# A scheduled attention and FFN kernel: batch 0's FFN spread later, batch 2's attention in two rounds

## The chip, the cores and the metric

One NeuronCore of one Trainium2 chip. The metric is device time in microseconds (us) of one execution, as the median of several runs. Engines: PE is TensorE (its weight loads are shown apart as PEld), DVE is VectorE, ACT is ScalarE, POOL is GpSimd, SP is SyncE, which here issues all DMAs.

## What is computed

Eight batches of attention with 8 heads, 576 positions and head size 64, in which a score counts only if it is within `tau` of its row's maximum, and behind it a two-layer FFN (512 to 2048 to 512, SiLU between) over all 4608 rows, in float32:

```python
scores = scale * np.matmul(q, k.transpose(0, 1, 3, 2))
thresh = np.max(scores, axis=-1, keepdims=True) - tau
scores = np.where(scores >= thresh, scores, -1000000000.0)
attn = softmax(scores)
x = (attn @ v).transpose(0, 2, 1, 3).reshape(B * S, H * D)
h = x @ w_in
g = h * (1.0 / (1.0 + np.exp(-h)))
out = g @ w_out
```

## The kernel before

**Tiles.** Attention goes by tiles of 128 score rows against all 576 keys of a head; the two heads of a pair share the tile with the last 64 rows of each. There are 36 tiles a batch and 288 in all; in this text they are counted from 0. Per tile: PE writes scores (L468; L456 in batch 0), DVE takes the row maximum (L478), ACT the exponential (L488), DVE masks and sums (L497), the tile is scaled by the inverse sum (L515 on ACT or L511 on POOL), POOL splits it into two halves of float16 (`hl`, L523, L526, L529), and SP transposes it by DMA into `wT` (L539). Batch 0 instead transposes on PE (`tm` L407, `tl` L412) and copies the result out on ACT (L420, L421). When a head pair is done, PE multiplies by the values (L554; L430 in batch 0) and `av_post` writes the FFN's input `x16` (L572 on ACT, L573 on DVE).

**Rounds.** A batch either runs all its tiles pair by pair (kind `all`, query columns 0 to 287 and 288 to 575 as FFN ranges) or in two rounds over the four pairs: `low` with 256 query columns (4 tiles a pair) and `high` with the other 320 (5 tiles a pair). Two rounds let the FFN of the first range begin when the first round is done. Batch 0 always does this; batches named in `HALVED` (L41) do too. In each round of a halved batch a head's queries and keys are loaded (`load_qk`, L338 and L339, through SP) and split: keys on ACT and POOL (`split_k`, L362 and L364), queries on ACT and DVE (`split_q`, L353 and L354; only the round's columns).

**FFN units.** A range of columns gives 16 h units (12 matmuls of the first layer, L597, then L607, L608, L614, L615 on ACT and DVE in turn, into `gbuf`) and 16 o units (12 matmuls of the second layer, L630; every fourth is followed by an output copy L642 on ACT and its DMA L644). The ranges of batch 0, and the first of batch 1, list their h units before their o units; later ranges pair their h units with the o units of the range before.

**Pacing.** The main loop counts steps t, one per tile, with 12 empty steps (`GAP`) between batch 0's two rounds and one (`GAP1`) before batch 1; a tile's number is t less the empty steps before it. At each step it adds `rate` to a credit and emits one FFN unit for each whole credit. `rate` is set when a range becomes ready: for batch 0 from `RATES` (1.03 after the first round, 1.45 after the second), later so that the units in the list are 95% done when the next range comes.

**Scheduler.** The instructions are not run in the order of the loop. A scheduler with its own timing model sets each engine's order, by priorities that put scores, soft-max and the value product ahead of FFN units. `keep_in_program_order` pins the first matmul of a unit behind whatever PE instruction the loop emitted just before it; it is used for batches below `PACED` (L34).

Of the kernel before, what the change touches and what calls it, by code (L numbers as in the profile page):

```python
# [30 lines left out]
LOAD = 5  # L31
AV_LAG = 3
GAP, GAP1 = 12, 1
PACED = 1  # L34
RATES = (1.03, 1.45)
RATE = 0.95

W_PLAN = ((0, 0, 10, 13, 0), (16, 9, 22, 36, 0))
PRI_S, PRI_SOFT1, PRI_SOFT2 = 1600, 50, 200
PRI_AV = 1500  # L40
HALVED = (1,)  # L41

# [8 lines left out]
def attention_moe(  # L53
# [198 lines left out]
    def load_v(b, p):  # L252
        t = sb.tile([P, 2, 5, D], F32, tag="vraw", name=f"vraw_{b}_{p}", bufs=5)
        nc.sync.dma_start(out=t, in_=vL[b, :, 2 * p : 2 * p + 2])
        vraw[b, p] = t
# [3 lines left out]
    def vmax(b, p):  # L259
        if b == 0:  # L260
            if p == 0:
                vps.append(bank([P, P], "vps_0", 2))
            flat = vraw[b, p].rearrange("p o k d -> p (o k d)").bitcast(BF16)
            upper = flat.rearrange("p (c t) -> p c t", t=2)[:, :, 1]
            for j in range(5):
                part = upper[:, j * P : (j + 1) * P]
                nc.tensor.matmul(
                    vps[0], part, part, start=(p == 0 and j == 0), stop=(p == 3 and j == 4)
                )
            if p == 3:  # L270
                vmx[b] = const.tile([P, 1], F32, name="vmx_0", tag="vmx0")
                nc.vector.tensor_reduce(out=vmx[b], in_=vps[0], op=ALU.max, axis=AX.X)
            return
        if p == 0:
            vmx[b] = const.tile([P, NPAIR], F32, name=f"vmx_{b}", tag="vmx")
        nc.vector.tensor_reduce(
            out=vmx[b][:, p : p + 1], in_=vraw[b, p], op=ALU.max, axis=AX.XYZ,
            apply_absolute_value=True,
        )
# [31 lines left out]
    def split_v(b, p):  # L311
        t = vraw[b, p]
        s = vsc[b][:, 0:1]
        o = sb.tile([P, 2, 2, 5, D], F16, tag="v16", name=f"v16_{b}_{p}", bufs=4)
        nc.scalar.activation(o[:, 0], t, AF.Copy, scale=s)
        nc.vector.scalar_tensor_tensor(
            out=o[:, 1], in0=t, scalar=s, in1=o[:, 0], op0=ALU.mult, op1=ALU.subtract
        )
        v16[b, p] = o
# [124 lines left out]
    def scores(t):  # L444
        v, parts = tiles[t]
        s_ps = ps_s.tile([P, 2, 512], F32, tag="s", name=f"s_{t}")
        sps[t] = s_ps
        if v in direct:
            (h, i, _, _) = parts[0]
            qt, kt = direct[v]  # L450
            if visits[v][2] == "low":
                o = (h % 2) * 256 + i * P
            else:
                o = (h % 2) * 384 + (i - 2) * P
            for j in range(2):
                nc.tensor.matmul(  # L456
                    s_ps[:, j, :HALF], qt[:, o : o + P],
                    kt[:, j * HALF : (j + 1) * HALF], start=True, stop=True,
                )
            return  # L460
        seq = [
            (qstack[h % 2][:, qcol(h, i) : qcol(h, i) + P], kk)
            for h, i, _, _ in parts
            for kk in khl[h]
        ]
        for n, (lhs, kk) in enumerate(seq):
            for j in range(2):
                nc.tensor.matmul(  # L468
                    s_ps[:, j, :HALF], lhs, kk[:, j * HALF : (j + 1) * HALF],
                    start=(n == 0), stop=(n == len(seq) - 1),  # L470
                )

    def soft1(t):
        s_ps = sps[t]
        sm = sb.tile([P, 5], F32, tag="small", name=f"sm_{t}", bufs=4)
        w = sb.tile([P, S], F32, tag="w32", name=f"w32_{t}", bufs=4)
        negm = sm[:, 0:1]
        nc.vector.tensor_reduce(  # L478
            out=negm, in_=s_ps[:, :, :HALF], op=ALU.max, axis=AX.XY, negate=True
        )  # L480
        nc.vector.tensor_scalar(
            out=sm[:, 1:2], in0=negm, scalar1=-1.0, scalar2=ntau, op0=ALU.mult, op1=ALU.add
        )
        small[t] = sm
        wtile[t] = w
# [104 lines left out]
    def h_unit(b, c0, n, f, own=None):  # L590
# [4 lines left out]
        for c in range(NK):  # L595
            for lo_w, lo_x in ((0, 0), (0, 1), (1, 0)):
# [3 lines left out]
                )  # L600
                if b < PACED and k == 0:
                    tc.keep_in_program_order(mm)
# [20 lines left out]
    def o_unit(b, c0, n, d, quarter, own=None):  # L623
# [3 lines left out]
        for f in range(4 * quarter, 4 * quarter + 4):  # L627
            g = gt[b, c0, f]
            for k, (lo_w, lo_g) in enumerate(((0, 0), (0, 1), (1, 0))):
# [3 lines left out]
                )  # L633
                if b < PACED and f == 4 * quarter and k == 0:
                    tc.keep_in_program_order(mm)
# [12 lines left out]
    def h_units(b, c0, n, owns=(None,)):  # L648
        return [
            lambda f=f: h_unit(b, c0, n, f, owns[f % len(owns)]) for f in range(NF)  # L650
        ]

    def o_units(b, c0, n, owns=(None,)):
        return [
            lambda d=d, quarter=quarter: o_unit(b, c0, n, d, quarter, owns[d % len(owns)])
            for d in range(DM // P) for quarter in range(4)
        ]
# [3 lines left out]
    def moe_units(b, c0, n):  # L661
        if b == 0 and c0 == 0:
            return h_units(b, c0, n, (0, 2)) + o_units(b, c0, n, (0, 2))
        if b == 0 or (b == 1 and c0 == 0 and 1 in HALVED):
            return h_units(b, c0, n) + o_units(b, c0, n)
        out = []
        if held:
            for pair in zip(h_units(b, c0, n, (0, 1)), o_units(*held.pop(), (2,))):
                out.extend(pair)
        else:  # L670
            out = h_units(b, c0, n)
        held.append((b, c0, n))
        return out
# [3 lines left out]
    for b in range(1, B):  # L677
        for kind in ("low", "high") if b in HALVED else ("all",):
            visits += [(b, p, kind) for p in range(NPAIR)]
    todo = {}  # L680
    def at(t, f):
        todo.setdefault(t, []).append(f)
# [42 lines left out]
    for b in range(B):  # L725
        u = start[b, 0]
        for p in range(NPAIR):
# [3 lines left out]
            elif b == 1:  # L731
                at(u + 5 * p - 20, lambda p=p: load_v(1, p))
                at(u + 5 * p - 15, lambda p=p: vmax(1, p))
                at(u + (4 if 1 in HALVED else 9) * p + 4, lambda p=p: split_v(1, p))
            else:
                pace, first = (4, 24) if b in HALVED else (9, 40)
                at(u + pace * p - first, lambda b=b, p=p: load_v(b, p))
# [4 lines left out]
    def pri(offset, f):  # L742
        def g():
            if offset == 0:
                return f()
            with tc.high_priority(offset=offset):
                return f()

        return g
# [25 lines left out]
    rate = 0.0  # L775
# [6 lines left out]
    def step_unit():  # L782
        p = units.pop(0)()
        run_posts()
        post.append(p)

    def live(t):
        return 0 <= t < NT and tiles[t] is not None
# [3 lines left out]
    while t < NT + 8 or units or ready or held:  # L792
        while ready and ready[0][0] <= t:
            _, b, c0, n = ready.pop(0)
            units.extend(moe_units(b, c0, n))
            nxt = [r[0] for r in ready if r[0] > t + 1]
            rate = len(units) / max(1, (nxt[0] if nxt else NT + 8) - t)
            rate *= RATE
            if b == 0:
                rate = RATES[0 if c0 == 0 else 1]  # L800
        if held and not ready and not units and t >= NT + 8:
            units.extend(o_units(*held.pop()))
        if t >= first_high + 20:
            turn[1] = 3
        if live(t):
            pri(PRI_SOFT1, lambda: soft1(t))()
        if live(t + 1):
            pri(PRI_S, lambda: scores(t + 1))()
        if live(t - 1):
            soft2b(t - 1)  # L810
        if live(t):
            pri(PRI_SOFT1, lambda: soft1b(t))()
        if live(t - 1) and tiles[t - 1][0] not in direct:
            soft3(t - 1)
        if live(t - 2) and tiles[t - 2][0] in direct:
            soft3(t - 2)
        for f in todo.pop(t, []):
            f()
        credit += rate
        if t >= NT:  # L820
            credit = max(credit, 4.0)
        if units and credit >= 1:
            step_unit()
            credit -= 1
        if live(t):
            pri(PRI_SOFT2, lambda: soft2(t))()
        for v, p, c0, n in avs.pop(t, []):
            b = visits[v][0]
            if v in direct:
                a_ps = av_direct(v, p)  # L830
            else:
                a_ps = pri(PRI_AV, lambda v=v, p=p, c0=c0, n=n: av(v, p, c0, n))()
            run_posts()
            scale = xscale if v in direct else 2.0**-12
            post.append(lambda b=b, p=p, c0=c0, n=n, a_ps=a_ps, scale=scale: av_post(b, p, c0, n, a_ps, scale))
        while units and credit >= 1:
            step_unit()
            credit -= 1
        if not units:
            credit = 0.0  # L840
            run_posts()
        t += 1
# [44 lines left out]
```

## Time and profile before

| | us |
|---|---|
| median of three timed runs (1227.8 to 1229.81) | 1228.99 |
| the profiled execution | 1226.58 |
| its span, first to last instruction | 1224.8 |
| PE busy | 1155.2 (94%) |
| DVE busy | 920.7 (75%) |
| ACT busy | 808.4 (66%) |
| POOL busy | 694.6 (57%) |

Busy shares are averages over stages with different limits, so the span is cut into stages at tile boundaries. A row of a stage gives the time in which each engine was busy; what is missing to the stage's length is idle time of that engine. The idle time of the engine that sets the end is what can be won.

### The profile page before, as it was taken

What the parts mean: (1) busy time and instruction counts of PE and PEld (TensorE: products, weight loads), DVE (VectorE), ACT (ScalarE), POOL (GpSimd) and SP (SyncE); (2) the same over time, 40 slices, a digit from 0 to 9 for tenths busy, and PEclk for the clock granted to TensorE, in tenths of its full rate; (3) what the DMA queues carried; (4) which work ended last, traced back from release to release, by engine and by line L of the source; (5) the groups of instructions that cost most, each with busy time, mean ns of one, the idle gap of its engine ahead of it and who ended that gap; (6) DMA issues with size and microseconds to landing.
All of it is one profiled execution on the core that took longest, in us unless ns stands there. A gap on an engine that the chain in (4) does not pass through costs nothing.

```text
span 1224.8 us, 27015 instructions
## 1 busy us (share of the span) xinstructions
PE 1155.2 (94%) x9474; PEld 902.3 (74%) x9474; DVE 920.7 (75%) x2625; ACT 808.4 (66%) x1519; POOL 694.6 (57%) x888
## 2 busy tenths in 40 slices
PE   6778998999999899999999999999999999999998
PEld 4546685777876677777877777787788877777777
DVE  7987949968989788899888888896788867333330
ACT  6679846967868676777777677785777756333331
POOL 2264226987877786877878658781787567000000
PEclk9999999999999999999999999999999999999999
DMA  9740127787896787787777748772888357100000
GB/s 313 264 133 28 51 58 180 155 167 159 152 172 128 168 148 136 146 154 172 142 145 145 162 96 171 142 136 82 137 159 141 84 103 122 26 11 16 15 11 25
DMA packets 340887, 151.73 MB, mean 124 GB/s; under 512 B 305936, under 2 KB 317200, under 8 KB 340752
## 3 DMA queue, kind: packets, MB, share of 16 engines
q1 hardware_dynamic: 340752, 150.01, 57.9%
q8 instruction: 75, 1.23, 0.4%
q14 instruction: 60, 0.49, 0.1%
HBM read 66.19 MB, written 9.44 MB: 62 GB/s over the span
## 4 chain that ended last, share of the span: by engine, by line
PE 54%; DVE 16%; DMA 9%; POOL 8%; ACT 6%; issue 6%; SPq 0%; POOLq 0%; ACTq 0%; DVEq 0%
PE o L630 20%; PE h L597 18%; PE s L468 7%; PE a L554 6%; DMA wT<-hl 5%; DVE w L497 4%; DVE sm L478 3%; DVE qstack L354 3%; POOL hl L526 2%; POOL hl L523 2%; ACT w L515 2%; ACT w L488 1%; PE s L456 1%; DMA vraw<-in_vL 1%; POOL wst L229 1%
## 5 line engine op out<-in xcount | busy, mean ns | idle before, releaser
L597 PE MATMUL h<-x,wst 128*128 128x288 f16 (+2 forms) x3072 | 423.4, 287 | 8.9 <-DVE gbuf L615 6.8
L630 PE MATMUL o<-gbuf,wst 128*128 128x288 f16 (+2 forms) x3072 | 418.5, 286 | 2.2 <-ACT wst L642 0.7
L597 PEld LDWEIGHTS <-wst 128*128 128x128 f16 x3072 | 292.1, 98 | 99.1 <-issue 21.0
L630 PEld LDWEIGHTS <-wst 128*128 128x128 f16 x3072 | 293.2, 98 | 82.3 <-issue 5.3
L526 POOL TENSOR_TENSOR hl<-w,hl 128x512 f16<-128x512 f32 x252 | 303.8, 1206 | 11.9
L523 POOL TENSOR_SCALAR hl<-w 128x576 f16<-128x576 f32 x252 | 171.7, 684 | 178.3 <-ACT w L515 140.6
L497 DVE SCALAR_TENSOR_TENSOR w<-s,sm,w 128x576 f32<-128x576 f32 x288 | 231.8, 812 | 47.1 <-ACT w L488 44.2
L488 ACT ACTIVATE w<-s,sm 128x576 f32<-128x576 f32 x288 | 210.9, 740 | 77.1 <-DVE sm L478 34.0
L478 DVE TENSOR_REDUCE sm<-s 128x1 f32<-128x576 f32 x288 | 215.2, 751 | 47.1 <-PE s L468 38.2
L515 ACT ACTIVATE w<-w,sm 128x576 f32<-128x576 f32 x266 | 201.6, 771 | 46.2 <-DVE sm L505 45.3
L607 ACT ACTIVATE th<-h,msc 128x288 f32<-128x288 f32 (+2 forms) x256 | 127.5, 499 | 110.4 <-PE h L597 109.2
L608 DVE SCALAR_TENSOR_TENSOR h<-th,h 128x288 f32<-128x288 f32 (+2 forms) x256 | 116.2, 456 | 109.9 <-ACT th L607 108.2
L468 PE MATMUL s<-khi,qstack 128*128 128x288 f32 x560 | 143.4, 336 | 9.3 <-DVE w L497 8.6
L614 ACT ACTIVATE gbuf<-h 128x288 f16<-128x288 f32 (+2 forms) x256 | 104.1, 408 | 71.9 <-DVE h L608 70.5
L615 DVE SCALAR_TENSOR_TENSOR gbuf<-h,gbuf 128x288 f16<-128x288 f32 (+2 forms) x256 | 115.3, 451 | 41.6 <-ACT gbuf L614 41.1
L554 PE MATMUL a<-wT,v 128*64 128x288 f16 (+2 forms) x1568 | 118.6, 292 | 12.9 <-DMA wT<-hl 12.7
L468 PE MATMUL s<-klo,qstack 128*128 128x288 f32 x560 | 120.7, 296 | 0.0
L364 POOL TENSOR_TENSOR klo<-kraw,khi 128x576 fp32r<-128x576 f32 x64 | 93.0, 1453 | 45.1 <-ACT khi L362 32.5
L554 PEld LDWEIGHTS <-v 128*64 128x64 f16 x1568 | 86.7, 111 | 36.8 <-issue 26.6
L468 PEld LDWEIGHTS s<-khi,qstack 128*128 128x128 f32 x560 | 87.3, 189 | 29.3 <-issue 15.3
L468 PEld LDWEIGHTS s<-klo,qstack 128*128 128x128 f32 x560 | 90.0, 188 | 0.8 <-issue 0.2
L529 POOL TENSOR_TENSOR hl<-w,hl 128x64 f16<-128x64 f32 x252 | 90.3, 358 | 0.0
(101 smaller groups left out, 905.5 us busy)
## 6 DMA issues: line engine op xcount, KB each, us to landing
kraw<-in_kT SPq DMA_DIRECT2D x128, 144.0 KB, 2.9
qraw<-in_qT SPq DMA_DIRECT2D x96, 144.0 KB, 3.0
vraw<-in_vL SPq DMA_DIRECT2D x32, 320.0 KB, 3.8
out_t<-wst SPq DMA_DIRECT2D x48, 144.0 KB, 2.1
gbuf<-in_w_in SPq DMA_DIRECT2D x12, 512.0 KB, 7.2
wT<-hl SPq DMA_TRANSPOSE x280, 3.3
wraw<-in_w_out SPq DMA_DIRECT2D x8, 512.0 KB, 4.5
gbuf<-in_w_out SPq DMA_DIRECT2D x8, 512.0 KB, 4.9
```

The lines of the kernel that those rows point to most:

```text
L468: nc.tensor.matmul(s_ps[:, j, :HALF], lhs, kk[:, j * HALF : (j + 1) * HALF], start=(n == 0), stop=(n == len(seq) - 1),)
L478: nc.vector.tensor_reduce(out=negm, in_=s_ps[:, :, :HALF], op=ALU.max, axis=AX.XY, negate=True)
L488: nc.scalar.activation(wtile[t].rearrange("p (j c) -> p j c", j=2), sps[t][:, :, :HALF], AF.Exp, bias=small[t][:, 0:1],)
L497: nc.vector.scalar_tensor_tensor(out=w3, in0=s_ps[:, :, :HALF], scalar=sm[:, 1:2], in1=w3, op0=ALU.is_ge, op1=ALU.mult, accum_out=sm[:, 2:3],)
L515: nc.scalar.activation(w, w, AF.Copy, scale=r)
L523: nc.gpsimd.tensor_scalar(out=fl[:, 0:S], in0=w, scalar1=1.0, scalar2=1.0, op0=ALU.mult, op1=ALU.mult)
L526: nc.gpsimd.tensor_tensor(out=fl[:, 640:1152], in0=w[:, 0:512], in1=fl[:, 0:512], op=ALU.subtract)
L554: nc.tensor.matmul(a_ps[odd * D : (odd + 1) * D, :n], vt[:, lo_v, odd, kv, :], wT[v, b * H + 2 * p + odd][:, kw, c0 - base : c0 - base + n ...
L597: mm = nc.tensor.matmul(ph[:, :n], wi(c, f, lo_w), x16[b, lo_x][:, c, c0 : c0 + n], start=(k == 0), stop=(k == 11),)
L607: nc.scalar.activation(th[:, :n], ph[:, :n], AF.Tanh, scale=moe_sc[b][:, 0:1])
L608: nc.vector.scalar_tensor_tensor(out=ph[:, :n], in0=th[:, :n], scalar=1.0, in1=ph[:, :n], op0=ALU.add, op1=ALU.mult,)
L630: mm = nc.tensor.matmul(ps[:, :n], wo(f, d, lo_w), g[:, lo_g, :n], start=(f == 0 and k == 0), stop=(f == NF - 1 and k == 2),)
```

## The change

`RATES` for batch 0 go from 1.03 and 1.45 units a step to 0.25 and 1.75. A new constant `TOP` caps the rate of batches 1 and 2 at 1.75. `PACED` goes from 1 to 3, so units of batches 1 and 2 are pinned in PE's order too. `HALVED` gets batch 2, which then runs in a `low` and a `high` round like batch 1; its values are loaded 24 steps ahead of the batch at 4 steps a pair, where it was 40 steps ahead at 9, and are split 4 steps apart, where it was 9. By the loop's arithmetic 8 units of batch 0 are emitted before its second range is ready (tile 39), where it was 32. Lines from L34 on are one later in the changed kernel, and three later behind the cap.

```diff
-PACED = 1
-RATES = (1.03, 1.45)
+PACED = 3
+TOP = 1.75
+RATES = (0.25, 1.75)
...
-HALVED = (1,)
+HALVED = (1, 2,)
...
             if b == 0:
                 rate = RATES[0 if c0 == 0 else 1]
+            elif b < PACED:
+                rate = min(rate, TOP)
```

On ACT, in batch 0's second round, around the exponentials of tiles 28 and 29 (`w_40` and `w_41`, named by the step; `th` and `gbuf` are an h unit, `wT` copies and `wst` splits belong to batch 0's attention and to the weights). Before:

```order
L488 ACTIVATE w_40_1620<-s_1587,sm_1619 128x576
L224 ACTIVATE wst<-wst,o_w_sc 128x512
L421 ACTIVATE wT_3_1525<-tl_1560 128x128
L614 ACTIVATE gbuf<-h_0_9_1173 128x256
L420 ACTIVATE wT_4_1635<-tm_1628 128x4x128
L224 ACTIVATE wst<-wst,o_w_sc 128x512 x2
L607 ACTIVATE th_0_10_1271<-h_0_10_1215,msc_770 128x256
L421 ACTIVATE wT_3_1525<-tl_1597 128x128
L488 ACTIVATE w_41_1657<-s_1623,sm_1656 128x576
L420 ACTIVATE wT_4_1635<-tm_1665 128x4x128
L607 ACTIVATE th_0_11_1315<-h_0_11_1258,msc_770 128x256
L421 ACTIVATE wT_4_1635<-tl_1633 128x128
```

Now:

```order
L489 ACTIVATE w_40_1368<-s_1332,sm_1367 128x576
L422 ACTIVATE wT_3_1296<-tl_1317 128x128
L225 ACTIVATE wst<-wst,o_w_sc 128x512
L421 ACTIVATE wT_4_1383<-tm_1376 128x4x128
L225 ACTIVATE wst<-wst,o_w_sc 128x512 x2
L422 ACTIVATE wT_3_1296<-tl_1342 128x128
L489 ACTIVATE w_41_1390<-s_1371,sm_1389 128x576
L608 ACTIVATE th_0_4_1423<-h_0_4_1349,msc_770 128x256
L615 ACTIVATE gbuf<-h_0_4_1349 128x256
L421 ACTIVATE wT_4_1383<-tm_1398 128x4x128
L422 ACTIVATE wT_4_1383<-tl_1381 128x128
```

Where units 9, 10 and 11 of batch 0's first range stood, there is unit 4 alone; the attention rows are the same.

On ACT again, where batch 0 gives way to batch 1 (the exponential of tile 35 and, as `w_49`, that of tile 36). Before:

```order
L614 ACTIVATE gbuf<-h_0_15_1434 128x256
L642 ACTIVATE wst<-o_0_0_1475,msc_770 128x256
L642 ACTIVATE wst<-o_0_1_1638,msc_770 128x256
L421 ACTIVATE wT_6_1834<-tl_1832 128x128
L488 ACTIVATE w_47_1909<-s_1858,sm_1908 128x576
L420 ACTIVATE wT_6_1834<-tm_1863 128x4x128
L421 ACTIVATE wT_6_1834<-tl_1868 128x128
L488 ACTIVATE w_49_1986<-s_1945,sm_1985 128x576
```

Now:

```order
L489 ACTIVATE w_47_1588<-s_1544,sm_1587 128x576
L421 ACTIVATE wT_6_1534<-tm_1593 128x4x64
L422 ACTIVATE wT_6_1534<-tl_1554 128x128
L489 ACTIVATE w_49_1651<-s_1625,sm_1650 128x576
L421 ACTIVATE wT_7_1602<-tm_1593 128x4x64
```

The output copies of two finished blocks of o units stood ahead of tile 35's exponential, so eight o units had to be done by then; now no o unit of batch 0 is done there.

On POOL, early in batch 2's first (now) round (`klo` is a key split, `hl` a tile's split). Before:

```order
L364 TENSOR_TENSOR klo_4144<-kraw_17_4062,khi_4142 128x576
L526 TENSOR_TENSOR hl_4056<-w_83_3980,hl_4056 128x512
L529 TENSOR_TENSOR hl_4056<-w_83_3980,hl_4056 128x64
L523 TENSOR_SCALAR hl_4105<-w_84_4046 128x576
L526 TENSOR_TENSOR hl_4105<-w_84_4046,hl_4105 128x512
L529 TENSOR_TENSOR hl_4105<-w_84_4046,hl_4105 128x64
L523 TENSOR_SCALAR hl_4136<-w_85_4095 128x576
```

Now:

```order
L365 TENSOR_TENSOR klo_3715<-kraw_17_3568,khi_3713 128x576
L527 TENSOR_TENSOR hl_3708<-w_83_3635,hl_3708 128x512
L530 TENSOR_TENSOR hl_3708<-w_83_3635,hl_3708 128x64
L365 TENSOR_TENSOR klo_3817<-kraw_18_3718,khi_3815 128x576
L524 TENSOR_SCALAR hl_3752<-w_84_3698 128x576
L527 TENSOR_TENSOR hl_3752<-w_84_3698,hl_3752 128x512
L530 TENSOR_TENSOR hl_3752<-w_84_3698,hl_3752 128x64
```

The next head's key split comes one tile later instead of four tiles later; over the batch there are 16 key splits, where there were 8.

## Rows read from the trace of the kernel before

**Rows 1.** Windows A to F: length; busy of PE, PEld, DVE, ACT, POOL; clock.

```profile
0.00:75.00 75.00, 55.04 (x327) 36.46 (x327) 62.99 (x193) 49.27 (x94) 18.88 (x30) 0.93 0.84 280
75.00:159.00 84.00, 71.72 (x470) 51.50 (x471) 66.14 (x194) 68.42 (x149) 38.71 (x40) 0.98 0.14 42
159.00:306.00 147.00, 136.81 (x1105) 105.24 (x1104) 117.00 (x336) 103.44 (x195) 103.81 (x129) 0.99 0.70 147
306.00:529.00 223.00, 208.23 (x1756) 164.14 (x1754) 194.73 (x566) 163.53 (x294) 172.47 (x221) 0.98 0.79 150
529.00:1035.00 506.00, 496.95 (x4279) 396.59 (x4277) 427.16 (x1222) 363.84 (x660) 356.21 (x464) 1.00 0.69 135
1035.00:1225.00 190.00, 186.43 (x1547) 148.41 (x1544) 52.65 (x119) 59.92 (x131) 4.49 (x8) 1.00 0.08 20
```

**Rows 2.** Windows inside B (two) and C (two), same columns.

```profile
100.00:141.00 41.00, 36.58 (x231) 26.31 (x231) 36.22 (x98) 39.79 (x89) 11.30 (x11) 0.96 0.10 27
141.00:159.00 18.00, 17.73 (x131) 13.50 (x131) 13.24 (x43) 9.77 (x25) 6.97 (x8) 1.00 0.25 69
159.00:172.00 13.00, 13.00 (x121) 11.82 (x119) 2.76 (x7) 3.65 (x8) 0.75 (x1) 1.00 0.07 21
...
182.00:228.00 46.00, 39.16 (x290) 27.42 (x289) 43.18 (x117) 35.48 (x67) 33.70 (x41) 0.96 0.73 162
```

**Rows 3.** PE's timeline in B: start us, us, instruction, [idle before <-releaser].

```profile
99.84 0.47 PE L412 MATMUL tl<-ident,w 128*128 128x128 f32 x1 [2.46 <-ACT wT L421]
100.53 2.29 PE L456 MATMUL s<-kd,gbuf 128*128 128x288 f32 x4 [0.22 <-DVE w L497]
```

**Rows 4.** PE's timeline in D, one hole.

```profile
361.06 1.91 PE L554 MATMUL a<-wT,v 128*64 128x288 f16 x28 [2.32 <-DMA wT<-hl]
```

**Rows 5.** Windows: the first half of D and the two stretches after D.

```profile
306.00:417.00 111.00, 101.50 (x869) 80.89 (x867) 99.69 (x285) 82.03 (x148) 84.75 (x107) 0.98 0.78 152
...
529.00:648.00 119.00, 117.24 (x1015) 93.51 (x1013) 106.27 (x308) 89.60 (x162) 91.77 (x119) 1.00 0.76 154
648.00:773.00 125.00, 120.40 (x1041) 96.11 (x1039) 108.01 (x302) 90.06 (x163) 90.12 (x116) 1.00 0.69 143
```

**Rows 6.** PE's timeline at the end of batch 0 and in F.

```profile
158.79 9.23 PE L630 MATMUL o<-gbuf,wst 128*128 128x256 f16 x83
...
1113.96 3.10 PE L597 MATMUL h<-x,wst 128*128 128x288 f16 x24
1116.90 3.23 PE L630 MATMUL o<-gbuf,wst 128*128 128x288 f16 x25
```

**Rows 7.** Groups by line and shape, whole span: xcount | busy us, mean ns | idle before.

```profile
L364 POOL TENSOR_TENSOR klo<-kraw,khi 128x576 fp32r<-128x576 f32 x64 | 93.0, 1453 | 45.1 <-ACT khi L362 32.5 <-DMA out_t<-wst 10.0 <-DMA wT<-hl 1.8
L354 DVE SCALAR_TENSOR_TENSOR qstack<-qraw,gate,qstack 64x576 fp32r<-64x576 f32 x48 | 58.2, 1212 | 3.7 <-ACT qstack L353 1.9 <-DMA wT<-hl 0.4
L354 DVE SCALAR_TENSOR_TENSOR qstack<-qraw,gate,qstack 64x320 fp32r<-64x320 f32 x8 | 6.4, 804 | 0.3
L354 DVE SCALAR_TENSOR_TENSOR qstack<-qraw,gate,qstack 64x256 fp32r<-64x256 f32 x8 | 6.3, 783 | 0.7 <-ACT qstack L353 0.5
L607 ACT ACTIVATE th<-h,msc 128x256 f32<-128x256 f32 x32 | 15.3, 480 | 3.9 <-PE h L597 3.7
L608 DVE SCALAR_TENSOR_TENSOR h<-th,h 128x256 f32<-128x256 f32 x32 | 13.4, 420 | 5.6 <-ACT th L607 5.6
L615 DVE SCALAR_TENSOR_TENSOR gbuf<-h,gbuf 128x256 f16<-128x256 f32 x32 | 13.3, 414 | 0.4 <-ACT gbuf L614 0.3
L614 ACT ACTIVATE gbuf<-h 128x256 f16<-128x256 f32 x32 | 12.5, 392 | 3.2 <-DVE h L608 3.1
```

**Rows 8.** DVE's timeline at the start of C.

```profile
169.12 0.82 DVE L497 SCALAR_TENSOR_TENSOR w<-s,sm,w 128x576 f32<-128x576 f32 x1 [9.05 <-ACT w L488]
```

**Rows 9.** Timelines of DVE's narrow query split and of POOL in C.

```profile
195.70 0.90 DVE L354 SCALAR_TENSOR_TENSOR qstack<-qraw,gate,qstack 64x256 fp32r<-64x256 f32 x1
...
195.16 1.16 POOL L526 TENSOR_TENSOR hl<-w,hl 128x512 f16<-128x512 f32 x1
```

## The prediction

> **What bounds the kernel now.** From the page's totals (PE busy for 1155.2 of 1224.8 us, no other engine over 920.7) PE is the first suspect, but a total hides where it waits. So I cut the span at tile boundaries (a tile's time is that of its row maximum on DVE). Stage A is tiles 0 to 15, B tiles 16 to 35 (batch 0's second round), C tiles 36 to 75 (batch 1 and the first four of batch 2), D tiles 76 to 143 (the rest of batch 2 and all of batch 3), E tiles 144 to 287, F what is left when attention has ended. In the windows of these stages PE is idle for 20.0, 12.3, 10.2, 14.8, 9.1 and 3.6 us, 70 us in all [rows 1]. In F PE does nothing but FFN and its only idle time is at the end. PE is thus the bound, the change takes no FFN or attention work from it, and every unit not done early is done later at PE's price. So the change is worth what it does to PE's idle time, and I price each stage by how its length changes.
>
> Who holds PE up differs by stage. In the first half of B it is ACT: 39.79 of 41 us busy, against 36.22 for DVE and 36.58 for PE; in the last 18 us of B PE itself is full [rows 2]. PE's worst hole there, 2.46 us, waits for an ACT copy [rows 3]. C begins with 13 us in which PE is full of FFN and DVE does 2.76 us of work; then in 46 us DVE is busy for 43.18 [rows 2]. In D PE waits, for 2.32 us in one place, for a transposing DMA [rows 4]; in D's first half DVE is at 99.69 and PE at 101.50 of 111 us, while the two stretches after D have PE at 117.24 of 119 and 120.40 of 125 [rows 5].
>
> **The change part by part: prices.** A unit is 12 matmuls. At 288 columns, 24 matmuls take from 1113.96 to 1116.90: 1.47 us a unit. I scale by columns: 1.31 at 256 and 1.63 at 320; the row of 83 matmuls of 256 columns in 9.23 us, which holds the last one's tail too, agrees [rows 6]. An h unit of 256 columns costs besides 0.480 + 0.392 us on ACT and 0.420 + 0.414 us on DVE [rows 7]; an o unit costs these engines a quarter of one output copy.
>
> **What moves.** Counting units between tiles in PE's order of both kernels: B goes from 18.1 units to 6.0 (10 h and 2.1 o fewer, all of 256 columns), C from 54.9 to 45.4 (3.1 of 256 columns more, 12.6 o of 320 fewer), D from 86.0 to 98.7, E and F from 353.0 to 361.9. In PE time: B -15.9, C -16.5, D +16.7, E and F +15.7 us. A is untouched.
>
> B: in the ACT-bound 41 us seven of the ten h units go, 7 x 0.87 = 6.1 us of ACT. In the full-PE 18 us three h and 2.1 o go, 6.7 us of PE; but DVE has 13.24 us of work there, 3 x 0.83 less without them, so some 5 us can be won. Sum -11. The bounds: -5 (part of ACT's share, the rest lost to latency) and -15.9 (all of PE's time; ACT's 68.42 - 8.7 us would still fit). I take -11, the sum from the windows; PE's idle time in B grows by 5.
>
> C: PE falls to 136.81 - 16.5 = 120.3 us, and DVE stays at 117.0 + 0.9 (one h unit more) = 117.9. Where the two were as level, in the first half of D, DVE filled 0.90 and PE 0.914. DVE's 117.9 at 0.914 is 129 us, so -18. Where this comes from can be seen: the 13 us full of FFN hold a hole of 9.05 us on DVE [rows 8], because a small transpose stands behind seven o units (the 83 matmuls [rows 6]) in PE's order. The bounds: -9 (that hole closes, nothing else) and -23 (DVE filled to 0.95).
>
> D: PE rises to 224.9 us. Batch 2 in two rounds adds the second key split of 8 heads, 8 x 1.453 = 11.6 us on POOL and as many copies on ACT. The query split becomes 16 narrow instead of 8 wide: on DVE 8 x (0.783 + 0.804 - 1.212) = +3.0 us [rows 7]. All this is spread over the end of C and the first half of D. Five more h units put some 4.5 us on DVE and on ACT. DVE is then near 202 and POOL near 184 us, under PE's 224.9. The 16 more key loads and 8 more sets of query loads stand on SP's queue, in order with the transposes; no row prices that, and it is kept in the upper bound. PE filled 0.974 of the two stretches after D, with DVE at 0.88 of them [rows 5]; at 0.974 D takes 231 us, +8. The bounds: +5 (0.985, the better of the two) and +17.8 (D's present 0.934 stays).
>
> E and F are full of PE and grow by the 15.7 us that they take over. Pinning batches 1 and 2 binds little: units stand later in PE's order than the loop emits them (50.7 done at tile 76, where it has emitted 73), so I price it at nothing; if the backlog were gone, D's upper bound is its price.
>
> Sum: -11 - 18 + 8 + 15.7 = -5.3 us. The profiled execution took 1226.58 us for a span of 1224.8; it becomes 1221.3. The median of the timed runs, 1228.99, lies 2.4 us above the profiled one; carried over, I forecast **1223.7 us**.
>
> **A rule on the shared port.** The narrow query split at 195.70 took 0.90 us and ended at 196.60, 0.28 us after POOL's instruction of 195.16 had ended at 196.32 [rows 9]; of the mean of 0.783 us, 0.5 is thus mostly a wait for POOL, and the +3.0 us on DVE is eight more such waits. The Trainium skill, page "SBUF — State Buffer", section "Who interferes with whom", says that a DVE instruction with two SBUF inputs contends with a GpSimd instruction that reads SBUF. It speaks against this change, which puts more of both into batch 2. By it eight waits of 0.5 us, 4 us, would come on DVE where the rows' means give 3.0; the trace agrees.
>
> **The rivals.** (1) *PE starves early.* The loop emits a quarter of a unit a step until tile 39. If attention in B and C is held by latency (maximum, exponential, masking, scaling one after the other), taking FFN out shortens little and PE idles. With B at -5 and C at -9, and +8 and +15.7 behind, the sum is +9.7: **1238.7**, slower. It decides as soon as B and C together shorten by less than 23.7 us. For it: PE's hole in B that waits for an ACT copy. Against it: ACT is busy for 39.79 of 41 us, so work and not latency holds there.
> (2) *Batch 2's second split takes the gain.* If D keeps its 0.934, the sum is +4.5: **1233.5**. For it: POOL is at 84.75 of 111 us in batch 2 and gets 11.6 more. Against it: at 96.4 of 111 it would still have 13% to spare.
> (3) *The clock.* In A, where there is no FFN, the mean granted clock is 0.93; in B and C 0.98 and 0.99 [rows 1]. If B and C fall to 0.93, C's PE loses 0.06 x 129 = 7.7 us, becomes the bound at 128 us, and filled to 0.93 takes 138: sum +3.3, **1232**. The four score matmuls after the hole of 2.46 us took 2.29 us [rows 3], and the 41 us around them have 0.96 [rows 2]. The Trainium skill, "TensorE: Matmul & The Clock Gate", section "HAM oscillation — how this bites in real kernels", says that PE's waits make its clock fall again and again. E, with waits of its own, keeps 1.00 [rows 1], so the trace bears this out only in part.
> (4) *Nothing but a shift.* B and C give back just the 23.7 us that D to F take: **1229**.
> (5) *More than forecast.* B wins two more, D's holes close and C runs at 0.95 of DVE: -13 - 23 + 5 + 15.7 = -15: **1214**.
> That the order does not move is excluded by the order itself.
>
> **How the numbers follow.** Forecast (1218 to 1226.5) 0.41; rival 1 0.15; rival 2 0.08; rival 3 0.05; rival 4 0.17; rival 5 0.14. A measurement of this kernel can tell about 0.2% (2.5 us) from no change. Faster by more: 0.41 + 0.14 = 0.55; within: 0.17; slower by more: 0.15 + 0.08 + 0.05 = 0.28. The range goes down to 1211, under rival 5, and up to 1237, through rival 1: about 0.03 is left out below and 0.1 above.
>
> **What would show it.** In the changed profile: tile 36 about 11 us earlier (before: 159), tile 76 some 29 us earlier (before: 306), then a stage D near 231 us with PE at 0.97, and E and F together 16 us longer. PE's idle time should be near 65 us, B's greater by 5 and D's less by 8 or 9. No run of o units should stand before a transpose at tile 36. It would be wrong if B and C shorten by less than 24 us (rival 1), if D's share stays at 0.93 with DVE or POOL named before PE's holes (rival 2), or if the clock before 300 us is near 0.93 (rival 3).

## Result and the profile after

The changed kernel takes 1246.41 us (median; 1245.47 to 1248.28), the kernel before 1228.67: a ratio of 1.0146, 95% interval 1.0128 to 1.0163. It is slower by 1.5%, where 1223.7 us, a gain of 0.4%, had been forecast. The profiled execution of the changed kernel, the slowest of its four, took 1248.28 us for a span of 1246.5.

Cut at the same tiles as [rows 1] (16, 36, 76, 144 and the end of attention), the windows of the changed kernel read as follows; the columns are those of [rows 1].

```profile
0.00:75.00 75.00, 54.02 (x332) 36.30 (x333) 63.77 (x193) 49.70 (x95) 19.73 (x31) 0.93 0.87 283
75.00:154.00 79.00, 62.68 (x333) 41.06 (x333) 60.88 (x177) 63.78 (x134) 38.05 (x39) 0.89 0.14 41
154.00:289.00 135.00, 118.69 (x977) 92.79 (x974) 119.91 (x338) 102.58 (x193) 107.21 (x133) 0.97 0.77 156
289.00:531.00 242.00, 226.48 (x1912) 179.79 (x1911) 205.32 (x582) 171.66 (x317) 174.10 (x226) 0.98 0.75 150
531.00:1062.00 531.00, 517.13 (x4428) 410.91 (x4426) 432.52 (x1231) 368.04 (x672) 353.07 (x462) 1.00 0.67 129
1062.00:1247.00 185.00, 181.16 (x1504) 144.22 (x1501) 51.49 (x117) 58.63 (x128) 5.57 (x8) 1.00 0.09 21
```

The work moved as the order said. What did not follow is the time:

| stage | before | after | change | forecast | PE idle before | PE idle after |
|---|---|---|---|---|---|---|
| A, to tile 16 | 75 | 75 | 0 | 0 | 20.0 | 21.0 |
| B, tiles 16 to 35 | 84 | 79 | -5 | -11 | 12.3 | 16.3 |
| C, tiles 36 to 75 | 147 | 135 | -12 | -18 | 10.2 | 16.3 |
| D, tiles 76 to 143 | 223 | 242 | +19 | +8 | 14.8 | 15.5 |
| E and F | 696 | 716 | +20 | +15.7 | 12.6 | 17.7 |

(The last window runs half a microsecond past the span's end; idle times here include it.) B and C gave back 17 us in place of 29, and D to F took 39 in place of 24. PE's idle time went from 70 to 87 us and its busy time, for as many matmuls (9474 records in both profiles), from 1155.2 to 1160.2.

Inside C there are new holes. PE's timeline of the changed kernel (start us, us, instruction, idle before and who ended it):

```profile
176.04 4.45 PE L598 MATMUL h<-x,wst 128*128 128x256 f16 x24 [4.28 <-DVE gbuf L616]
...
185.11 2.78 PE L598 MATMUL h<-x,wst 128*128 128x256 f16 x24 [1.53 <-DVE gbuf L616]
...
192.78 2.32 PE L598 MATMUL h<-x,wst 128*128 128x256 f16 x12 [3.37 <-DVE gbuf L616]
```

and what DVE does up to the first of them:

```profile
168.85 0.42 DVE L609 SCALAR_TENSOR_TENSOR h<-th,h 128x256 f32<-128x256 f32 x1
...
170.68 0.88 DVE L317 SCALAR_TENSOR_TENSOR v<-vraw,v_sc,v 128x640 f16<-128x640 f32 x1
...
171.54 1.67 DVE L317 SCALAR_TENSOR_TENSOR v<-vraw,v_sc,v 128x640 f16<-128x640 f32 x2
174.52 1.14 DVE L317 SCALAR_TENSOR_TENSOR v<-vraw,v_sc,v 128x640 f16<-128x640 f32 x1
175.58 0.74 DVE L616 SCALAR_TENSOR_TENSOR gbuf<-h,gbuf 128x256 f16<-128x256 f32 x2
```

An h unit of batch 0 that had its first DVE step at 168.85 gets its second at 175.58, behind the four value splits of batch 1; the next h units wait for it, and PE has no o unit to do instead. Before, all 16 h units were done in B, and o units, which need nothing of DVE, stood here. The 24 matmuls at 176.04 take 4.45 us where the forecast's price of 1.31 us a unit makes it 2.6: behind the hole the granted clock is at half, 0.50 from 176.2 to 179.6.

What these holes cost is another matter. Tiles 40 to 45, before and now, and behind them the rest of C as it is now:

```profile
182.80:212.00 29.20, 24.37 (x175) 16.65 (x173) 26.57 (x71) 20.75 (x39) 20.66 (x25) 0.94 0.73 173
...
167.00:190.00 23.00, 16.47 (x125) 11.89 (x124) 22.87 (x65) 17.32 (x34) 14.66 (x18) 0.93 0.71 179
190.00:289.00 99.00, 91.72 (x773) 73.20 (x773) 86.20 (x243) 75.32 (x138) 85.60 (x109) 0.98 0.83 161
```

The first two holes lie in a stretch that became 6 us shorter and in which DVE is busy for 22.87 of 23 us. There DVE sets the pace, and PE's idle time is what is left over. C's time went elsewhere: tiles 36 to 45 together went from 52.9 to 36.1 us, and tiles 46 to 75 from 93.8 to 99.0.

### The profile page after: what moved, and what is told of

Same layout as the page of the kernel before. It is cut to its first block, busy times and chain, and to the rows that moved or that the text cites. A ratio compares the mean times of both kernels' runs of the same rounds, so it can differ in the third digit from the quotient of the medians.

```text
span 1246.5 us, 27131 instructions
## 1 busy us (share of the span) xinstructions
PE 1160.2 (93%) x9474; PEld 905.1 (73%) x9474; DVE 933.9 (75%) x2633; ACT 814.4 (65%) x1535; POOL 697.7 (56%) x896
## 4 chain that ended last, share of the span: by engine, by line
PE 56%; DVE 16%; DMA 9%; ACT 7%; POOL 6%; issue 5%; SPq 1%; POOLq 0%; ACTq 0%; DVEq 0%
PE o L631 22%; PE h L598 20%; PE s L469 7%; PE a L555 6%; DMA wT<-hl 4%; DVE w L498 4%; DVE sm L479 3%; DVE qstack L355 3%; POOL hl L527 2%; POOL hl L524 2%; DMA vraw<-in_vL 1%; ACT w L516 1%; DVE h L609 1%; DMA gbuf<-in_w_in 1%; DVE gbuf L616 1%
## 5 line engine op out<-in xcount | busy, mean ns | idle before, releaser
L598 PE MATMUL h<-x,wst 128*128 128x288 f16 (+2 forms) x3072 | 426.9, 289 | 16.8 <-DVE gbuf L616 15.7
L527 POOL TENSOR_TENSOR hl<-w,hl 128x512 f16<-128x512 f32 x252 | 300.7, 1193 | 11.0
L365 POOL TENSOR_TENSOR klo<-kraw,khi 128x576 fp32r<-128x576 f32 x72 | 103.6, 1439 | 70.0 <-ACT khi L363 69.6
L555 PE MATMUL a<-wT,v 128*64 128x288 f16 (+2 forms) x1568 | 117.1, 291 | 12.7 <-DMA wT<-hl 12.3
L530 POOL TENSOR_TENSOR hl<-w,hl 128x64 f16<-128x64 f32 x252 | 87.8, 348 | 0.0
```

The lines of the kernel that those rows point to most:

```text
L527: nc.gpsimd.tensor_tensor(out=fl[:, 640:1152], in0=w[:, 0:512], in1=fl[:, 0:512], op=ALU.subtract)
L555: nc.tensor.matmul(a_ps[odd * D : (odd + 1) * D, :n], vt[:, lo_v, odd, kv, :], wT[v, b * H + 2 * p + odd][:, kw, c0 - base : c0 - base + n ...
L598: mm = nc.tensor.matmul(ph[:, :n], wi(c, f, lo_w), x16[b, lo_x][:, c, c0 : c0 + n], start=(k == 0), stop=(k == 11),)
```

## Experiments

Three theories: R, that the low first rate takes work out of B and C which was done there beside other waits; H, that batch 2's second round costs more than it gives; P, that the pins or the cap do. Ratios are to the kernel before on the same chip, with the 95% interval.

**The rates alone.**

```diff
-RATES = (1.03, 1.45)
+RATES = (0.25, 1.75)
```

> The kernel before with batch 0's rates alone changed (0.25 and 1.75 units a step). Theory R (the early stages pay): by the two traces, tile 76 came 16.8 us earlier in the changed kernel while 32.4 us of PE time were moved behind it; so the rates alone should lose 10 to 17 us, 1239 to 1246. Theory H (the second round of batch 2 pays): the rates alone are within 4 us of the kernel before. Theory P (the pinning and the cap pay): the same, within 4 us.

1241.56 us, 1.0118 (1.0085 to 1.0150). Theory R. Its windows at the tile boundaries:

```profile
74.00:152.00 78.00, 61.08 (x335) 39.80 (x337) 60.99 (x178) 63.53 (x134) 38.86 (x40) 0.93 0.15 44
152.00:288.00 136.00, 118.73 (x967) 91.90 (x964) 119.45 (x337) 101.75 (x191) 105.84 (x131) 0.96 0.75 156
288.00:529.00 241.00, 223.17 (x1858) 174.06 (x1857) 202.59 (x571) 167.04 (x300) 168.05 (x221) 0.97 0.71 139
529.00:1055.00 526.00, 518.97 (x4491) 417.15 (x4489) 428.63 (x1235) 367.76 (x676) 352.91 (x462) 1.00 0.67 131
```

33.8 us of PE's FFN time left B and C (priced as in the forecast: 105.9 us before, 72.1 now). B and C shortened by 17 us (231 to 214); D to F, up to the span's end, grew by 33 (919 to 952). So behind tile 76 a moved unit costs its full PE time; in front of it, leaving saved half.

**Batch 2 in two rounds alone.**

```diff
-HALVED = (1,)
+HALVED = (1, 2,)
```

> The kernel before with batch 2 in two rounds and nothing else. Theory R: within 5 us of the kernel before, either way (1224 to 1234). Theory H: the added key and query splits and the earlier value splits cost 10 to 18 us, 1239 to 1247. Theory P: within 5 us.

1224.6 us, 0.9973 (0.9951 to 0.9995). Theory H falls: the two rounds win a little. It is the one complete version tried here that beats the kernel before, by 0.3%.

**Pins and cap alone**, with old rates and batch 2 in one round.

```diff
-PACED = 1
+PACED = 3
+TOP = 1.75
...
+            elif b < PACED:
+                rate = min(rate, TOP)
```

> The kernel before with batches 1 and 2 pinned in PE's order and capped at 1.75, old rates, batch 2 in one round. Theory R and theory H: within 5 us (1224 to 1234). Theory P: 10 us or more slower, with PE's new holes between tiles 76 and 143, where 75 units stand instead of 86.

1233.67 us, 1.0040 (1.0021 to 1.0059): slower, by less than theory P wanted.

**The changed kernel with the old rates.**

```diff
-RATES = (0.25, 1.75)
+RATES = (1.03, 1.45)
```

> The changed kernel with batch 0's old rates (1.03 and 1.45), the rest as changed. Theory R: most of the loss goes, 1226 to 1234. Theory H and theory P: most of the loss stays, 1240 or more.

1227.76 us, 1.0008 (0.9989 to 1.0027). The whole loss goes with the rates: theory R again.

**The second rate alone.**

```diff
-RATES = (1.03, 1.45)
+RATES = (1.03, 1.75)
```

> The kernel before with batch 0's second rate alone changed (1.45 to 1.75 units a step), the first at 1.03. If the first rate carries the loss of the rates, this is within 4 us of the kernel before. If the burst after batch 0 carries it, 6 us slower or more.

1228.52 us, 0.9997 (0.9973 to 1.0021). It is the first rate, 0.25, that costs.

**Half the shift.**

```diff
-RATES = (1.03, 1.45)
+RATES = (0.5, 1.75)
```

> The kernel before with rates 0.5 and 1.75: 13 instead of 18 units stand in stage B and 19 instead of 25 h units in stage C's order. Theory S (starvation: every unit taken out of B and C saves about half of its PE time there and costs all of it later): 15 us of PE time leave B and C in place of 34, so the loss is near half of that with 0.25: 1234 to 1238. Theory V (the loss comes from batch 0's h units meeting batch 1's value splits on DVE in C): only 3 of them are left to meet, the loss is nearly gone, 1227 to 1232.

1230.74 us, 1.0020 (0.9992 to 1.0048). Not half the loss: within the noise, none or little. Its windows for B and C:

```profile
74.00:154.00 80.00, 67.85 (x418) 47.66 (x417) 64.69 (x191) 67.87 (x147) 38.09 (x39) 0.96 0.15 43
154.00:291.00 137.00, 123.97 (x1028) 95.39 (x1027) 117.39 (x328) 99.08 (x181) 107.45 (x133) 1.00 0.80 160
```

15.0 us of PE time left B and C, and they are 217 us long, 14 less than before. The first 15 us were thus given back nearly whole; the further 19 us of the rate 0.25 shortened B and C by 3 more. This looks like a floor; the runs below ask what it is.

**Idle matmuls in B** in the place of the FFN's.

```diff
+    def filler(t):
+        ph = bank([P, 512], f"fill_{t}", 2)
+        for k in range(7):
+            mm = nc.tensor.matmul(
+                ph[:, :256], wi(0, 0, 0), x16[0, 0][:, 0, 0:256], start=True, stop=True
+            )
+            if k == 0:
+                tc.keep_in_program_order(mm)
...
+        if first_high <= t < first_high + 20:
+            filler(t)
```

> Rates 0.25 and 1.75 as in the run with the rates alone, and in stage B seven idle matmuls a tile whose result nobody reads (140 in all, 15 us of PE at full clock, what the FFN's units there took). Theory K (the clock: PE, without FFN, drops to half its clock in B, and the slower transposes and scores hold attention): the spells at half clock in B go from 10 to 17 us to near 3, and B gets no longer or even shorter than 78 us. Theory S with PE as the limit of B: B goes back to 84 us or more and the total rises by 5 to 10 us to 1247 to 1252. Theory L (latency and the other engines hold B, PE's time is free there): B stays within 2 us of 78 us, total within 4 us of 1241.6, whatever the clock does.

1244.44 us, 1.0122 (1.0076 to 1.0168), as with the rates alone. B with the idle matmuls (14 of the 140 fall into C):

```profile
75.50:152.00 76.50, 69.36 (x458) 51.22 (x458) 60.55 (x180) 63.39 (x133) 36.81 (x37) 0.96 0.14 41
```

B is 76.5 us long against 78 without them, though PE is busy 8.3 us longer and idle for 7.1 us in place of 16.9. PE's time in B was free within the 2 us that theory L allowed. So what made B 6 us longer in the kernel before is not the units' matmuls; what is left of a unit is its steps on ACT and DVE. The clock is bounded too, though less strictly: added work and a better clock act against each other here, and only their sum, -1.5 us, is measured. The granted clock was at half for 6.8 us of B in place of 10.2, which is worth 1.7 us of PE's work.

**Only the o units late**: batch 0's h units keep their place.

```diff
-        credit += rate
+        if t >= first_high + 24 or len(units) > NF:
+            credit += rate
```

> The kernel before with batch 0's 16 h units where they were and only its 16 o units of the first range held back until tile 40. Stage B keeps its order but for two o units. Theory V: no h unit is moved, so C's holes behind DVE don't come, and the loss is small, 1226 to 1232. Theory S: 18.9 us of PE time are moved out of C, the time there falls by about half, and the loss is 6 us or more: 1235 to 1240.

1234.69 us, 1.0049 (1.0021 to 1.0077), between what the two theories wanted.

```profile
75.00:161.00 86.00, 72.47 (x472) 50.99 (x470) 67.78 (x198) 69.79 (x155) 37.29 (x38) 0.98 0.13 37
161.00:292.00 131.00, 114.90 (x926) 88.07 (x926) 115.15 (x318) 95.76 (x172) 106.38 (x134) 0.95 0.85 166
```

21.6 us of FFN left (units are done in the order of the list, so all that stand behind the o units came later too); B and C are 217 us, 14 less. No h unit meets the value splits here, yet PE's idle time in C is 16 us as in the changed kernel, and in tiles 40 to 45 DVE is busy for 23.0 of 24.0 us again. So the meeting of h units and value splits on DVE is where the holes of the changed kernel lie, but not their cause alone: attention keeps DVE full there in any case.

**The same 16 o units left out**, in the kernel before and then with the new rates. In both, batch 0's first range has no o units, so its 256 output columns aren't computed.

```diff
-            return h_units(b, c0, n, (0, 2)) + o_units(b, c0, n, (0, 2))
+            return h_units(b, c0, n, (0, 2)) + [lambda: (lambda: None)] * NF
```

> The kernel before with the 16 o units of batch 0's first range left out altogether (192 of the 6144 FFN matmuls, 21 us of PE at full clock; those output columns aren't written). It asks what these units cost where they stand, at tiles 35 to 44. Theory S (they stood in time that PE would have spent waiting): it saves under 13 us, 1216 to 1228. If they were on the path, as the forecast took them to be, it saves 16 to 21 us: 1207 to 1212.

1216.39 us, 0.9901 (0.9872 to 0.9930): 11 us saved for 21 us of PE time. Where they stood, half of the time of these units was free.

> The kernel with the rates alone changed (1241.6), and the same 16 o units left out, which there stand at tiles 48 to 60 and push all that follows. Theory S: they are on the path there and leaving them out saves 16 to 22 us, 1220 to 1226, at least 6 us more than in the kernel before. If their place doesn't matter, both save the same within 4 us.

1230.0 us against 1241.56 with the rates alone: 11.6 us saved, the same, and not the 16 to 22 that theory S wanted. The theory had taken all of these units' time to be on the path in their new place. The stages say where it was not:

```profile
152.00:285.00 133.00, 113.28 (x867) 83.89 (x863) 120.33 (x339) 100.05 (x188) 107.43 (x134) 0.94 0.78 160
```

By the FFN matmuls that the traces show in each stage, priced as before, 9.9 us of FFN are gone from C and 11.1 us from D to F. C is 3 us shorter than with the rates alone (136), D to F are 10 us shorter (952 to 942). So C was at its floor and the units there were free, and behind tile 76 the full price held. Within D to F, D was 15 us shorter and E 5 us longer; why it fell so stays open.

**The pins alone.**

```diff
-PACED = 1
+PACED = 3
```

> The kernel before with batches 1 and 2 pinned in PE's order and no cap. The forecast priced the pinning at nothing: within 2.5 us of the kernel before. If the pinning and not the cap carries the 5 us that the two together cost, 1231 to 1236, with PE's idle time between tiles 76 and 143 near 19 us instead of 15; if it is the cap, 1226 to 1231.

1243.66 us, 1.0122 (1.0097 to 1.0147), above all that was expected. The pins cost the kernel before 16 us, and the cap beside them takes 10 us of that back (1233.67). Tiles 76 to 143, then 144 to the end of attention, against [rows 1]:

```profile
305.00:525.00 220.00, 198.44 (x1650) 155.76 (x1649) 195.34 (x562) 160.31 (x286) 173.40 (x222) 0.96 0.77 152
525.00:1051.00 526.00, 513.92 (x4382) 407.96 (x4380) 430.41 (x1226) 366.38 (x667) 355.02 (x463) 1.00 0.68 130
```

Only 76.8 units stand between tiles 76 and 143 (86.0 before), PE is idle there for 21.6 us, and what was not done there lengthens the next stage by 20 us.

**Batches 1, 2 and 3 in two rounds.**

```diff
-HALVED = (1,)
+HALVED = (1, 2, 3)
```

> The kernel before with batches 1, 2 and 3 in two rounds. Batch 2 in two rounds alone won 0.3%. If its gain is FFN that starts 20 tiles sooner and fills PE's holes, a third batch adds little, as PE's idle time behind tile 144 is 9 us in all: 1221 to 1228. If the second split of keys costs POOL and DVE more than it gives there, 1228 to 1236.

1232.46 us, 1.0034 (1.0021 to 1.0048), in the range expected if the third batch costs more than it gives: 8 us against batch 2 alone.

**The changed kernel without pins.**

```diff
-PACED = 3
+PACED = 1
...
-            elif b < PACED:
+            elif b < 3:
```

> The changed kernel without the pins on batches 1 and 2, with the cap. The pins alone cost the kernel before 16 us. If they cost the changed kernel too, this is 1232 to 1240. If the backlog of units that the low rate makes takes the pins' effect away, as the forecast had it, it stays within 3 us of 1246.

1243.62 us, 1.0137 (1.0111 to 1.0163): within 3 us of the changed kernel. With the backlog, the pins bind little.

**The changed kernel without the cap.**

```diff
-TOP = 1.75
+TOP = 99.0
```

> The changed kernel without the cap of 1.75, with the pins. In the order 108 units stand between tiles 76 and 143 instead of 99. Without pins and backlog the cap was worth 11 us (pins alone +16, pins and cap +5). If it works by itself, this is 1252 or more; if the cap only mends what the pins do to a kernel without backlog, it is within 4 us of 1246 or faster.

1242.78 us, 1.0144 (1.0105 to 1.0183): no change either.

**New rates and two rounds, neither pins nor cap.**

```diff
-RATES = (1.03, 1.45)
+RATES = (0.25, 1.75)
...
-HALVED = (1,)
+HALVED = (1, 2,)
```

> The new rates and batch 2 in two rounds, neither pins nor cap. If the parts add up (rates +13.5, two rounds -3.5), 1234 to 1241, and the pins and the cap carry the rest of the changed kernel's loss.

1242.55 us, 1.0142 (1.0108 to 1.0176), above the 1234 to 1241 of parts that add up. It is the changed kernel's loss, so pins and cap carry none of it. The gain of the two rounds doesn't appear beside the new rates.

**Two rounds and a first rate of 0.75.**

```diff
-RATES = (1.03, 1.45)
+RATES = (0.75, 1.45)
...
-HALVED = (1,)
+HALVED = (1, 2,)
```

> Batch 2 in two rounds, old second rate, first rate 0.75: 16 h units stay in stage B as before, and 6 units of C go later. If C's floor is reached only below some 15 us moved out, the 8 us moved here are given back whole and the two rounds keep their 3.5 us: 1221 to 1227. If any unit moved out of C costs, 1228 to 1232.

1227.11 us, 1.0003 (0.9986 to 1.0019), just above what was expected if the shift is free. It is 2.5 us slower than two rounds alone, and the two intervals overlap a little: whether the 8 us moved here cost 3 us or nothing is not shown.

## Why the prediction was wrong, by its steps

The runs that move units out of B and C, side by side (PE's FFN time in their order at the forecast's unit prices; their length by single profiles. Profiles of kernels with the old rates, six in all, have B and C between 231 and 234 us, five with the new rates between 212.6 and 214.2, so a difference under 3 us says nothing):

| run | FFN time in B and C | moved out | length of B and C | saved there |
|---|---|---|---|---|
| before | 105.9 | | 231 | |
| rate 0.75, two rounds | 98.0 | 7.9 | 227 | 4 |
| rate 0.5 | 90.9 | 15.0 | 217 | 14 |
| o units left out | 86.3 | 19.6 | 220 | 11 |
| o units late | 84.3 | 21.6 | 217 | 14 |
| changed kernel | 73.6 | 32.3 | 214 | 17 |
| rate 0.25 alone | 72.1 | 33.8 | 214 | 17 |
| rate 0.25 and idle matmuls | 72.4 | 33.5 | 212 | 19 |

**What bounds the kernel.** That PE sets the end and that a unit done later costs PE's full price was right: 33.8 us moved, 33 us more behind tile 76. The changed kernel's own profile has 39 us more there for 32.3 moved, but the same kernel without pins, without the cap and without both has 33 (D to F take 952 us in each of the three). What was missed is the other half of the same sentence: a unit done early is free as far as PE would have waited there. The forecast priced B and C as if nearly all of their FFN time were on the path (29 of 32 us); the runs show 212 to 220 us that attention needs there, and below some 217 us more FFN taken out hardly shortens them. The two stages differ: B gave back 5 of 15.9 us, C 12 of 16.5.

**B, -11 forecast, -5 measured.** Both terms were too large. The first, 6.1 us of ACT's work in the 41 us of [rows 2], brought 4 us: tiles 22 to 30 went from 38.5 to 34.6 us. Those 41 us hold two stretches with different limits. In tiles 22 to 25 ACT is full, before (13.68 of 14 us) and after (12.31 of 12.5). In tiles 26 to 30 DVE was as busy as ACT, and it is what stays, as these windows show before and now:

```profile
117.00:141.40 24.40, 21.12 (x144) 15.01 (x144) 23.50 (x61) 23.51 (x54) 3.68 (x4) 1.00 0.09 26
...
116.50:138.50 22.00, 16.41 (x80) 10.36 (x79) 21.51 (x51) 19.27 (x40) 3.07 (x3) 0.84 0.08 20
```

The second term, 5 us to be won in B's last 18 us where PE was full [rows 2], is the one that failed most: 7 us of FFN went, and the stretch shortened by 2.3 (17.7 to 15.4). PE was full there because FFN filled it, not because attention waited for it; 25 of the idle matmuls stand there and cost about 1 us. Tiles 16 to 21 took 1 us more, within their scatter (25 to 30 us over all the profiles). The lower bound of the range, -5, is what was measured, and the text gave it to the rival.

**C, -18 forecast, -12 measured.** The failing step is the share of 0.914, in two ways. It is PE's share of a stretch in which both engines had FFN to do [rows 5], and it was put on DVE's work; DVE's own share there, 0.90, and PE's 120.3 us at 0.914 both give 131 to 132 us, or -15 to -16. And the share did not carry over: in the changed C the busier engine, DVE, fills 119.9 of 135 us, 0.89, with PE at 0.88. The hole of 9.05 us on DVE [rows 8] did close, and tiles 36 to 45 gave back nearly the whole price, 16.8 us for 17.9 us of FFN. What is missing was lost in tiles 46 to 75, 5.2 us longer: 2.2 us are FFN that they took over, and PE's idle time grew from 4.5 to 7.3 us, with most of the hole of 3.37 us in it. The forecast named none of these holes: it counted one h unit more in C and didn't look at whose DVE work it would queue behind.

**D, +8 forecast, +19 measured.** PE's added work is right (226.5 us busy, 224.9 forecast). The failing step is that more FFN would fill D's holes, from 14.8 us down to 6. It stayed at 15.5. Over the sixteen experiments PE's idle time in D lay between 12 and 22 us while its FFN time in the order ranged from 112 to 164 us, so these holes don't come from a lack of FFN. In the changed kernel's D steps of DVE ended 11.2 us of them and the transposing DMA of [rows 4] 3.9. Both were named in the forecast and then priced as if a backlog could fill them.

**E and F, +15.7 forecast, +20 measured:** 5 us of that are idle time. The profile of the same kernel without pins has 711 us there, +15, so they may belong to this one execution; no run tells their cause apart.

**Pins at nothing** was right in the changed kernel, and for the reason given: without them it is 3 us or less faster. The same pins without a backlog cost 16 us, so the price belongs to the state of the queue and not to the edit.

**The second split's cost** (+3.0 us on DVE, 11.6 on POOL) was 6.4 us of query splits on DVE and 10.6 us of key splits on POOL, and it found room: D in the kernel with two rounds alone is 7 us longer and takes on 10.7 us of FFN time. Rival 2 is out as a cause, though D kept its share, 0.936, in the changed kernel: with the rates alone, without any second split, D's share is the same 0.93 (223.17 of 241 us).

**The shared port.** [rows 9] was misread. A query split of 256 columns took 0.48 us at its fastest in this trace (the one at 201.05), so of the mean of 0.783 us 0.3 and not 0.5 was a wait, and eight such waits are 2.4 us and not 4. The direction held: in the changed kernel seven of the 16 splits of 256 columns took over 0.9 us, and each of the seven ended 0.28 us after the end of an instruction of POOL.

**The rivals.** Rival 1 came nearest: its prices for B and C (-5 and -9) were near the measured -5 and -12, and its point of decision held, as B and C shortened by 17 us, less than 23.7. It had 0.15. Its sum of +9.7 was still short of the measured +17.7, because it took D at the forecast's +8. Its reason, latency, fits in part only. In the changed kernel no engine is over 0.84 busy in tiles 16 to 21 and 36 to 39; but in tiles 22 to 30 and 40 to 45 ACT or DVE is full, with work. So the argument against it (ACT at 39.79 of 41 us is "work and not latency") read ACT rightly. The mistake was to conclude that the stretch would shorten by all the work taken from ACT: it shortened until DVE, whose other work stayed, was full. Rival 3 was half right on the fact: up to tile 76 the granted clock fell from 0.97 to 0.94, in B from 0.98 to 0.89, in C only from 0.99 to 0.97. On the price it was not borne out: PE's busy time over the whole span, for as many matmuls, grew by 5.0 us and its idle time by 17, and in the run with idle matmuls a better clock and PE's added work together moved B by 1.5 us. What part of the idle time a slower PE caused elsewhere than in B, no run tells.

## What to carry to other kernels

Before moving work out of a busy stretch, ask how long the stretch would be with none of it: an engine that is full of filler says nothing about that, and only the part above this floor is won by moving. Look for the floor in stretches short enough to have one limit each: a mean over 41 us hid that ACT was full in the first part and DVE as full as ACT in the second. Idle instructions put in the place of moved ones, whose result nobody reads, tell in one run whether an engine's time was on the path. And the loss at the new place is certain when the engine is full to the end there: here the first 8 to 15 us moved cost between nothing and 3 us, and the next 19 us about 11.

## What had not been expected of the hardware

The first stage, A, holds the same work in all these kernels and still took 72.1 to 75.5 us from profile to profile, so single profiles don't resolve a difference of 3 us there. PE's spells at half clock are not tied to long holes alone: B of the changed kernel, with idle time of 16.3 us in pieces of 1.62 us and less, had a mean granted clock of 0.89, the lowest of any stage there.
